# FNet mixing and a SwiGLU block in one kernel: the loads of the first two batches in another order, products of the first stage rearranged, and a new plan

## The chip, the cores and the metric

One core of a Trainium2 chip runs the whole program. Its engines are TensorE (PE, with its weight loads as PEld), VectorE (DVE), ScalarE (ACT), GpSimd (POOL) and SyncE (SP, which here issues transfers only); each works through its own queue of instructions in order, and semaphores tie the queues together. The metric is device time in microseconds of one execution. The median of 3 runs of the kernel before is 598.35 us (598.19 to 599.81).

## The reference

The input x holds 8 batches of 3008 rows of 256 numbers. Each batch goes through a two-dimensional Fourier transform of which the real part is kept; the 24,064 rows that result go through a gated feed-forward block with 1536 hidden features.

```python
X = np.fft.fft(x, axis=1)
X = np.fft.fft(X, axis=2)
x = X.real.reshape(24064, 256)
g = x @ w_gate
silu = g * (1.0 / (1.0 + np.exp(-g)))
out = (silu * (x @ w_val)) @ w_out
```

## The kernel before, in words

**What is computed where.** The transform over the 256 columns is folded into the weights: the products of CD and SDt (cosines and sines over columns) with the raw weights give Wp and Wq, and Wm is a mirrored copy of Wq with a sign. The transform over the 3008 rows is done as folds (sums and differences of rows that share a cosine) followed by matmuls with the table Tab. Its results are Pt and Qt, one pair of 128-partition tiles for each block of columns. The real transform is symmetric, so only 1504 rows of each batch are computed; each yields an output row and its mirror (the "p" and "m" halves, hp and hm).

**Tiles and units.** The 12,032 computed rows are cut into 24 tiles (480 or 512 columns, the last is shorter). A tile has 12 units of 128 hidden features. A unit makes a gate g and a value v in PSUM from Pt and Qt (line 972), turns them into sv, sp, es and sg on ScalarE and VectorE, and multiplies them to hp (VectorE, line 1186, or GpSimd, line 1192) and hm (GpSimd, line 1183, two units at a time). Then twelve such products per block of 128 rows are summed by TensorE with Wo (line 1236), copied by ScalarE (line 1243) and stored from SyncE's queue (line 1249).

**Kinds.** A string of KINDS per tile (line 928) gives each unit a digit. Bit 1 ("seeded") lets ScalarE put the even part of the value into PSUM (line 1045) and copy it back (line 1107), instead of one pass on VectorE (line 1109). Bit 2 saves one matmul of TensorE's five and costs two passes on VectorE (lines 1088 and 1152). Higher values move a product from VectorE to GpSimd. "w" is the plain form of tile 0.

**The planner.** From tile 0 on the order in each queue isn't written by hand. Sched (line 767) takes every operation with an engine, an assumed duration and the keys that it reads and writes, and puts them in order by a wished time: TensorE's assumed clock plus SHIFT for the operation's class plus BIAS for its tile and class. BIAS comes from the table BIAS_ROWS, 24 rows of 17 numbers. LAG, W_AT (when the raw weights are assumed to be there), the prices of loads in run_loads (line 1297) and the start times in the last S.run are assumptions too. The instructions themselves wait only on real semaphores; the plan decides their order.

**Batches and loads.** Each batch has a long set of rows (XA, 128 partitions) and a short one (XC, 60 partitions and a middle row). Each has "rising" rows, read as blocks of 8 (load_a) or 4 (load_c) partitions that each take four quarters of the batch, and "falling" rows in four transfers, one per quarter. Batch 0 has its own code: rises of the long set (line 258), falls (fall_a, line 261, two from ScalarE's queue and two from SyncE's), rises of the short set (rises_c, line 264), its falls (line 267). For batch 1 the short set goes to partitions 64 on, and the second of each pair of rows has to be at partitions 0 on for the fold; the rising rows are copied there on the chip (line 169), the falling ones are loaded as two half-rows each (line 164). C1_ORDER and A1_ORDER write out the order of batch 1's loads: u a rising block, d and e falls, m the middle row, c the copy. SyncE keeps at most eight transfers in flight: each issue waits for the one eight before it.

**The first stage** (batch 0, written by hand, lines 435 to 650). place (line 435) brings the rising rows into the order of the falling ones by a matmul with putA or putC; VectorE adds them crosswise (cross, cross_halves), folds them (half_fold), ScalarE casts them (half_cast, line 497), GpSimd makes the odd differences (fold_d, line 494; then EOb, line 555), and TensorE accumulates half_folded (long set) and folded_c (short set) in acc. row0 adds the first row from CEa and CEc, which heads (line 461) writes on GpSimd. ScalarE copies one half of acc to od (line 514), and first_puts (line 631) writes Pt and Qt. Between these stand first_w (line 502), the first quarter of the weight products, and load_w (line 391), the raw weights on GpSimd's queue; the weight products of the other quarters (line 1442) are units' work in tile 0.

**Later batches.** GpSimd folds each batch's sets in fold_steps (lines 178 to 202, first X to SDf), in between its products; the results feed the transforms on TensorE (line 1394).

Of the kernel before, what the change touches and what calls it, by code (L numbers as in the profile page):

```python
# [19 lines left out]
def kernel(  # L20
# [101 lines left out]
    def up_block(b, j, n):  # L122
        return rows_at(b, 2 * j - 1, [[2 * D, n], [R * D, 4], [1, 2 * D]])
# [10 lines left out]
    C1_EARLY = 6  # L134
    C1_ORDER = "uuduuduuduuduumuueuueuece"
    A1_ORDER = "uuuuduuuuduuuuduuuud"

    def load_a(b, q):
        X3 = XA.rearrange("p a q d -> p a (q d)")
        res = ([lambda h=h: q.dma_start(out=X3[LA * h:LA * (h + 1), 0:4, :],  # L140
                                         in_=up_block(b, JA - LA * h, LA)) for h in range(NA)] +
                [lambda a=a: q.dma_start(out=X3[:, 4 + a, :], in_=down_set(b, a, JA, LA, NA)) for a in range(4)])
        return in_order(A1_ORDER, u=res[:NA], d=res[NA:]) if b == 1 else res
# [5 lines left out]
    def load_c(b, q):  # L149

        X3 = XC.rearrange("p a q d -> p a (q d)")
        p0 = 64 * (b % 2)
        pm = p0 + NCR
        r = slice(p0, p0 + NCR)
        ups = [lambda h=h: q.dma_start(out=X3[p0 + LC * h:p0 + LC * (h + 1), 0:4, :],
                                       in_=up_block(b, JC - LC * h, LC)) for h in range(NC_)]
        mid = [lambda: q.dma_start(out=XC[pm:pm + 1, 0:4, 1],
                                   in_=rows_at(b, 0, [[R * D, 1], [R * D, 4], [1, D]]))]
        if b != 1:
            return ups + [lambda a=a: q.dma_start(out=X3[r, 4 + a, :], in_=down_set(b, a, JC, LC, NC_))  # L160
                          for a in range(4)] + mid

        def down(a, k):
            q.dma_start(out=XC[0:NCR, 4 + a, 0] if k else XC[r, 4 + a, 0],
                        in_=rows_at(b, R * (a + 1) - 2 * JC + k, [[2 * LC * D, NC_], [-2 * D, LC], [1, D]]))

        downs = [[lambda a=a, k=k: down(a, k) for a in range(4)] for k in range(2)]
        return in_order(C1_ORDER, u=ups, d=downs[0], e=downs[1], m=mid,
                        c=[lambda: q.dma_start(out=XC[0:NCR, 0:4, 1], in_=XC[r, 0:4, 0])])

# [99 lines left out]
    fall_a(3, nc.scalar)  # L270
    fall_a(2, q)
    fall_a(1, nc.scalar)
    fall_a(0, q)
    rises_c(q)

# [204 lines left out]

    def half_folded(eo, a0, first):
        for q in range(2):
            for a in range(a0, a0 + 2):
                dst, rhs = set_cols(acc[eo][q], Tab[:, 0, q, eo], a)
                nc.tensor.matmul(dst, EOb[:, eo, a, q, :], rhs, start=first and a == a0, stop=False, skip_group_check=True)
# [51 lines left out]
    psC = place(XC0, putC, 2, ((psO, "o"),))  # L537
    half_cast(0, 0)
    for a in range(2, 4):
        nc.scalar.copy(FA[:, a, :, P + 1:D], psA[a][:, :, P + 1:D])  # L540
    half_cast(0, 2)
    nc.scalar.activation(Z0.rearrange("p q k d -> p (q k d)"), zero.to_broadcast([P, 6 * P]), AF.Copy)
# [15 lines left out]
    cross_halves(FC[:, 0], XC0, psC, 0)  # L558
    half_fold(0, EB[:, 0, 0], FC[:, 0], psC, 0)
    folded_c(0, 0)  # L560
    copies = [first_w(0, k, 1, p_.tile([P, T], F32, name=n_)) for k, (p_, n_) in enumerate(((psG, "g"), (psV, "v")))]
    cross_halves(FC[:, 1], XC0, psC, 1)
# [7 lines left out]
    for a in range(2):  # L570
        folded_c(1, a, True)
    half_folded(1, 0, False)
    load_w(1, (1,))
    heads(Ec0[:, 0], Ec0[:, 1], CEc)
    load_w(2, (0, 1))
# [107 lines left out]
    def rows(r0, n, step):  # L683
# [7 lines left out]
    C2_AT = 39  # L691
    A1_LOAD = 8
    ROW_1 = 12
# [48 lines left out]
    )  # L742
    BIAS = {(t, k): v for t, row in enumerate(BIAS_ROWS) for k, v in zip(SHIFT, row)}
    ES_BUFS = 2
# [9 lines left out]
    WM_ACT = ()  # L754
    W_AT = (0.0, 2.0, 3.2, 4.6)
    SIGN_AT = 8
# [163 lines left out]
    def pool_us(n):  # L920
# [14 lines left out]
        "001601031052",  # L935
        "300171700001",
        "331213005030",
        "010271031001",
        "34130b310300",
        "01b300700101",  # L940
        "21312101b300",
        "001371310011",
        "32120011b212",
        "10130b135030",
        "000135003170",
        "033170001011",
        "213b21011200",
        "103b10319610",
        "4030b13300b0",
        "616404563200",  # L950
        "143034169230",
        "706150233313",
    )
# [343 lines left out]
    def run_loads(n):  # L1297
        for what, k, fn in loads[:n]:
            up = k < (NA if what[0] == "A" else NC_)
            r, w, us, ring = [], [((what[0],), k)], 0.4 if up else 0.62, 0.57 if up or what[0] == "C" else 1.14  # L1300
            if what == ("A", 1):
                r = [(("C",), C1_ORDER.rindex("u"))]
                us, ring = (0.42, 0.75) if A1_ORDER[k] == "u" else (0.75, 1.1)
            if what == ("C", 1):
                us, ring = (0.48, 0.75) if C1_ORDER[k] == "u" else (0.95, 1.0)
                if C1_ORDER[k] == "c":
                    r = [(("C",), j) for j, o in enumerate(C1_ORDER) if o == "u"]
            S.add("SP", us, fn, r=r, w=w, after=[(("A",), "pre" if A1_ORDER[k] == "d" else "preW")] if what == ("A", 1) else [],
                  lat=2.5, ring=ring)
        del loads[:n]  # L1310
# [306 lines left out]
    for i, u in enumerate(units):  # L1617
# [48 lines left out]
    owork.run(len(owork.steps))  # L1666
    S.run({'DVE': 1.6, 'ACT': 1.0, 'POOL': 1.4, 'PE': 0.0, 'SP': 2.0})

# [29 lines left out]
```

## Time and profile before

| | |
|---|---|
| median of 3 runs | 598.35 us |
| the profiled execution, in all | 600.4 us |
| its span, first to last instruction | 598.6 us |
| granted TensorE clock | 0.999 |
| moved from or to HBM | 29.43 MB read, 24.65 MB written |

Rows of a timeline give the start, the duration, the engine and line, the operation, "out<-in" by the program's names, the shape, and in brackets how long the engine had been idle before it and what ended that wait. "SPq" and "POOLq" are the issuing side of SyncE and GpSimd, "POOL ... DMA_DIRECT2D" a transfer issued by GpSimd. In windows each engine has its busy time and in brackets its number of instructions; the last columns are TensorE's granted clock, the transfer engines' mean busy share and GB/s.

### The profile page before, as it was taken

How to read it: one execution, taken by the hardware profiler on the slowest of the kernel's cores; microseconds unless marked ns; L12 is line 12 of the kernel's file. 1: busy time of each engine (PE TensorE's matmuls, PEld its weight loads, DVE VectorE, ACT ScalarE, POOL GpSimd, SP SyncE). 2: the span in 40 equal slices, each digit the busy share in tenths (PEclk: the TensorE clock that was granted, in tenths of full speed). 3: DMA queues.
4: the chain of work that ended last, by engine and by line, in shares of the span. 5: the costliest groups of instructions: out<-in, count | busy, mean ns of one | idle time of the engine just before them, and what ended most of it. 6: DMA issues, size and time to landing. Idle time of an engine off the chain costs nothing.

```text
span 598.6 us, 12468 instructions
## 1 busy us (share of the span) xinstructions
PE 587.0 (98%) x3953; PEld 389.2 (65%) x4012; DVE 570.3 (95%) x1064; ACT 557.4 (93%) x1080; POOL 527.8 (88%) x486
## 2 busy tenths in 40 slices
PE   7999999999999999999999999999999999999997
PEld 5456666666666666666666666666666666666686
DVE  8989999999999999999999999999999999999993
ACT  8778989989998999999999999999999999999995
POOL 8977999999899999998999998897986868687772
PEclk9999999999999999999999999999999999999999
DMA  9956347454715523454127122046221202111212
GB/s 247 150 110 115 109 121 141 132 140 117 178 46 107 136 70 113 123 129 138 57 55 166 46 62 82 19 115 161 63 64 37 65 19 80 48 46 53 60 54 81
DMA packets 51082, 57.65 MB, mean 96 GB/s; under 512 B 7283, under 2 KB 38439, under 8 KB 51017
## 3 DMA queue, kind: packets, MB, share of 16 engines
q1 hardware_dynamic: 47433, 53.91, 35.2%
q0 software_dynamic: 3216, 2.36, 2.8%
q8 instruction: 31, 0.51, 0.4%
q10 hardware_dynamic: 368, 0.59, 0.3%
q14 instruction: 34, 0.28, 0.2%
HBM read 29.43 MB, written 24.65 MB: 90 GB/s over the span
## 4 chain that ended last, share of the span: by engine, by line
PE 71%; ACT 8%; DMA 6%; DVE 4%; POOL 3%; issue 3%; SPq 1%; ACTq 0%; POOLq 0%; DVEq 0%
PE o L1236 30%; PE g L972 19%; PE v L972 16%; DMA XA<-in_x_dram 5%; ACT sv L1159 2%; PE o L1394 2%; PE g L1394 2%; ACT v L1045 2%; ACT es L1107 1%; POOL hm L1183 1%; DVE sv L1175 1%; ACT sp L1084 1%; DVE hp L1186 1%; ACT sp L1156 1%; ACT ev L1243 1%
## 5 line engine op out<-in xcount | busy, mean ns | idle before, releaser
L1183 POOL TENSOR_TENSOR hm<-sv 128x1024 bf16<-128x1024 f32 (+2 forms) x137 | 254.7, 1862 | 44.1 <-ACT sv L1159 17.7
L1175 DVE SCALAR_TENSOR_TENSOR sv<-es,v 128x512 f32<-128x512 f32 (+2 forms) x262 | 173.6, 668 | 5.4 <-PE v L972 2.8
L1236 PE MATMUL o<-Wo,hm 128*128 128x256 bf16 (+1 forms) x1128 | 163.6, 273 | 0.3
L1236 PE MATMUL o<-Wo,hp 128*128 128x256 bf16 (+1 forms) x1104 | 159.7, 273 | 0.2
L1186 DVE TENSOR_TENSOR hp<-sp,v 128x512 bf16<-128x512 f32 (+2 forms) x233 | 154.2, 668 | 2.8 <-PE v L972 2.0
L1236 PEld LDWEIGHTS <-hm 128*128 128x128 bf16 (+2 forms) x1140 | 111.8, 98 | 57.9 <-issue 2.5
L1236 PEld LDWEIGHTS <-hp 128*128 128x128 bf16 (+2 forms) x1140 | 111.9, 98 | 55.8 <-issue 0.9
L1159 ACT ACTIVATE sv<-g 128x512 f32<-128x512 f32 (+2 forms) x179 | 116.7, 671 | 4.6 <-PE g L972 2.3
L1084 ACT ACTIVATE sp<-g 128x512 f32<-128x512 f32 (+2 forms) x179 | 110.5, 621 | 4.1 <-PE g L972 2.7
L972 PE MATMUL v<-Pt,Wp 128*128 128x512 bf16 (+2 forms) x288 | 105.4, 375 | 1.8 <-DVE hp L1186 0.5
L972 PE MATMUL g<-Pt,Wp 128*128 128x512 bf16 (+2 forms) x280 | 104.4, 374 | 0.9 <-ACT sv L1159 0.7
L1045 ACT ACTIVATE v<-bc,w 128x512 f32<-128x512 bf16 (+2 forms) x146 | 104.6, 717 | 0.4
L1109 DVE SCALAR_TENSOR_TENSOR es<-bc,w,v 128x512 f32<-128x512 bf16 (+2 forms) x128 | 92.6, 731 | 2.4 <-ACT bc L1595 0.8
L1107 ACT ACTIVATE es<-v 128x512 f32<-128x512 f32 (+2 forms) x146 | 90.0, 618 | 3.8 <-PE g L972 1.0
L972 PE MATMUL g<-Qt,Wq 128*128 128x512 bf16 (+2 forms) x247 | 90.5, 374 | 0.4
L972 PEld LDWEIGHTS <-Wp 128*128 128x128 bf16 x576 | 56.3, 98 | 27.8 <-DVE Wp L505 0.7
L972 PE MATMUL g<-Qt,Wm 128*128 128x512 bf16 (+2 forms) x186 | 69.8, 375 | 0.2
L1088 DVE SCALAR_TENSOR_TENSOR sg<-bc,w,g 128x512 f32<-128x512 bf16 (+2 forms) x95 | 68.4, 723 | 1.4 <-PE g L972 0.7
L1159 ACT ACTIVATE sv<-sg 128x512 f32<-128x512 f32 (+2 forms) x95 | 65.1, 692 | 0.2 <-DVE sg L1152 0.2
L1152 DVE SCALAR_TENSOR_TENSOR sg<-sg,g 128x512 f32<-128x512 f32 (+2 forms) x95 | 62.9, 662 | 1.5 <-PE g L972 0.8
L1156 ACT ACTIVATE sp<-g 128x512 f32<-128x512 f32 (+2 forms) x95 | 57.7, 608 | 5.5 <-DVE sg L1152 5.3
L972 PE MATMUL v<-Qt,Wm 128*128 128x512 bf16 (+2 forms) x159 | 59.4, 374 | 0.8 <-ACT es L1107 0.4
(218 smaller groups left out, 759.1 us busy)
## 6 DMA issues: line engine op xcount, KB each, us to landing
out_dram<-ev SPq DMA_DIRECT2D x96, 128.0 KB
XA<-in_x_dram SPq DMA_DIRECT2D x30, 256.0 KB
XA<-in_x_dram SPq DMA_DIRECT2D x112, 64.0 KB
XC<-in_x_dram SPq DMA_DIRECT2D x28, 120.0 KB
XC<-in_x_dram SPq DMA_DIRECT2D x105, 32.0 KB
bc<-br SPq DMA_DIRECT2D x19, 128.0 KB
St<-Fc SPq DMA_DIRECT2D x12, 128.5 KB
out_dram<-ev SPq DMA_DIRECT2D x12, 120.0 KB
```

The lines of the kernel that those rows point to most:

```text
L972: nc.tensor.matmul(ps[:, :n], Wt[:, gv, fs], src[:, :n], start=start, stop=stop, skip_group_check=True)
L1045: nc.scalar.activation(T_[kv][:, :w], bc[t][:, :w], AF.Copy, scale=w0[:, 1, f:f + 1])
L1084: nc.scalar.activation(sp_to()[:, :w], T_[kg][:, :w], AF.Silu)
L1088: nc.vector.scalar_tensor_tensor(T_[keg][:, :w], bc[t][:, :w], w0[:, 0, f:f + 1], T_[kg][:, :w], op0=Alu.mult, op1=Alu.add)
L1107: nc.scalar.activation(T_[kes][:, :w], T_[kv][:, :w], AF.Copy, scale=2.0 if on_pool(u) > 1 else 1.0)
L1109: nc.vector.scalar_tensor_tensor(T_[kes][:, :w], bc[t][:, :w], w0[:, 1, f:f + 1], T_[kv][:, :w], op0=Alu.mult, op1=Alu.add)
L1156: nc.scalar.activation(sp_to()[:, :wp], T_[kg][:, :wp], AF.Silu)
L1159: nc.scalar.activation(sv()[:, f % 2, w - 1::-1, 1], T_[kgm if by_dve else kg][:, :w], AF.Silu)
L1175: nc.vector.scalar_tensor_tensor(sv()[:, f % 2, w - 1::-1, 0], T_[kes][:, :w], 2.0, T_[kv][:, :w], op0=Alu.mult, op1=Alu.subtract)
L1183: nc.gpsimd.tensor_tensor(hts_(t)[1][:, f - 1:f + 1, :w], sv()[:, :, :w, 1], sv()[:, :, :w, 0], op=Alu.mult)
L1186: nc.vector.tensor_tensor(hts_(t)[0][:, f, :wp], T_[ksp][:, :wp], T_[kv][:, :wp], op=Alu.mult)
L1236: nc.tensor.matmul(st["ps"][:n, j, :], hts[t][minus][:, f, c:c + n], Wo[:, f, :], start=(f == 0), stop=(f == nF - 1))
```

## The change

1. Batch 0: rises_c is issued from SyncE before the last fall of that queue. (fall_a(1) is on ScalarE's queue and stays where it is there.)
2. First stage: half_cast of the second half stands ahead of ScalarE's two copies to FA; first_w products are spread between folded_c, half_folded and row0; half_folded(1) is cut in two, each part followed by its row0; VectorE's cast of Wp for the value goes ahead of the Qt passes and turn_signs behind them; heads for CEc goes ahead of GpSimd's load of the value weights.
3. Batch 1, short set: four falls whole instead of eight half-rows, and a second on-chip copy for their second rows; the order is four rising blocks to a fall.
4. Batch 1, long set: its rising blocks are planned from unit 6 and its falls from unit 8, behind one another instead of mixed, and no longer assumed to wait for the short set. Every batch's rising blocks go 0, 4, 8, 12, 1, 5, ... instead of 0, 1, 2, ...
5. The plan: a second BIAS_ROWS stands behind the first and replaces it (all 24 rows differ), KINDS differs in 16 of the 24 tiles, and W_AT, the load prices, one lag and the last S.run's start times have other numbers.

```diff
-    C1_ORDER = "uuduuduuduuduumuueuueuece"
+    C1_ORDER = "uuuuduuuuduuuuduuudmcc"
...
-                                         in_=up_block(b, JA - LA * h, LA)) for h in range(NA)] +
+                                         in_=up_block(b, JA - LA * h, LA)) for h in (4 * (i % 4) + i // 4 for i in range(NA))] +
...
+        downs = [lambda a=a: q.dma_start(out=X3[r, 4 + a, :], in_=down_set(b, a, JC, LC, NC_)) for a in range(4)]
         if b != 1:
-            return ups + [lambda a=a: q.dma_start(out=X3[r, 4 + a, :], in_=down_set(b, a, JC, LC, NC_))
-                          for a in range(4)] + mid
-
-        def down(a, k):
-            q.dma_start(out=XC[0:NCR, 4 + a, 0] if k else XC[r, 4 + a, 0],
-                        in_=rows_at(b, R * (a + 1) - 2 * JC + k, [[2 * LC * D, NC_], [-2 * D, LC], [1, D]]))
-
-        downs = [[lambda a=a, k=k: down(a, k) for a in range(4)] for k in range(2)]
-        return in_order(C1_ORDER, u=ups, d=downs[0], e=downs[1], m=mid,
-                        c=[lambda: q.dma_start(out=XC[0:NCR, 0:4, 1], in_=XC[r, 0:4, 0])])
+            return ups + downs + mid
+        return in_order(C1_ORDER, u=ups, d=downs, m=mid,
+                        c=[lambda: q.dma_start(out=XC[0:NCR, 0:4, 1], in_=XC[r, 0:4, 0]),
+                           lambda: q.dma_start(out=XC[0:NCR, 4:8, 0], in_=XC[r, 4:8, 1])])
...
     fall_a(2, q)
+    rises_c(q)
     fall_a(1, nc.scalar)
     fall_a(0, q)
-    rises_c(q)
...
-    def half_folded(eo, a0, first):
-        for q in range(2):
+    def half_folded(eo, a0, first, qs=(0, 1)):
+        for q in qs:
...
     half_cast(0, 0)
+    half_cast(0, 2)
     for a in range(2, 4):
         nc.scalar.copy(FA[:, a, :, P + 1:D], psA[a][:, :, P + 1:D])
-    half_cast(0, 2)
...
+    copies = [first_w(0, 0, 1, psG.tile([P, T], F32, name="g"))]
     folded_c(0, 0)
-    copies = [first_w(0, k, 1, p_.tile([P, T], F32, name=n_)) for k, (p_, n_) in enumerate(((psG, "g"), (psV, "v")))]
+    copies.append(first_w(0, 1, 1, psV.tile([P, T], F32, name="v")))
...
-    half_folded(1, 0, False)
+    copies.append(first_w(1, 0, 0, psO.tile([P, T], F32, name="o")))
+    heads(Ec0[:, 0], Ec0[:, 1], CEc)
     load_w(1, (1,))
-    heads(Ec0[:, 0], Ec0[:, 1], CEc)
...
-    for i in range(2):
-        row0(0, i, acc[1][i])
     copies[0]()
     copies[1]()
+    copies[2]()
+    half_folded(1, 0, False, (0,))
+    row0(0, 0, acc[1][0])
+    od1 = even_copy(1)
+    half_folded(1, 0, False, (1,))
+    row0(0, 1, acc[1][1])
+    copies.append(first_w(1, 1, 1, psO.tile([P, T], F32, name="o")))
+    first_puts(1, od1, (0,))
+    copies[3]()
     turn_signs()
-    od1 = even_copy(1)
-    copies += [first_w(1, k, k, psO.tile([P, T], F32, name="o")) for k in range(2)]
-    first_puts(1, od1, (0,))
-    for c in copies[2:4]:
-        c()
...
-    A1_LOAD = 8
+    A1_LOAD = (6, 8)
...
-    W_AT = (0.0, 2.0, 3.2, 4.6)
+    W_AT = (0.0, 3.0, 4.0, 5.2)
...
-        "06ww20001013",
-        "031303160011",
-        "000010312133",
-        "010210112012",
+        "42ww20003010",
+        "031003330001",
+        "101330110133",
+        "010210112013",
...
             if what == ("A", 1):
-                r = [(("C",), C1_ORDER.rindex("u"))]
-                us, ring = (0.42, 0.75) if A1_ORDER[k] == "u" else (0.75, 1.1)
+                r = []
+                us, ring = (0.45, 1.0) if A1_ORDER[k] == "u" else (0.75, 1.2)
             if what == ("C", 1):
-                us, ring = (0.48, 0.75) if C1_ORDER[k] == "u" else (0.95, 1.0)
+                us, ring = (0.48, 0.7) if C1_ORDER[k] == "u" else (0.65, 1.0)
                 if C1_ORDER[k] == "c":
-                    r = [(("C",), j) for j, o in enumerate(C1_ORDER) if o == "u"]
+                    side = "u" if k == C1_ORDER.index("c") else "d"
+                    us, r = 0.95, [(("C",), j) for j, o in enumerate(C1_ORDER) if o == side]
...
-    S.add("DMA", 0.01, lambda: None, w=[(("pq", 0), "Q")], lat=0.1)
+    S.add("DMA", 0.01, lambda: None, w=[(("pq", 0), "Q")], lat=0.6)
...
-        if i == A1_LOAD:
-            loads[0:0] = ((("A", 1), k, fn) for k, fn in enumerate(load_a(1, nc.sync)))
+        if i in A1_LOAD:
+            side = "ud"[A1_LOAD.index(i)]
+            loads.extend((("A", 1), k, fn) for k, fn in enumerate(load_a(1, nc.sync)) if A1_ORDER[k] == side)
...
-    S.run({'DVE': 1.6, 'ACT': 1.0, 'POOL': 1.4, 'PE': 0.0, 'SP': 2.0})
+    S.run({'DVE': 1.4, 'ACT': 0.8, 'POOL': 1.6, 'PE': 0.0, 'SP': 2.2})
```

More of the change, by code (lines that the diff above doesn't have):

```diff
@@ L742 @@
     )
+    BIAS_ROWS = (
[24 rows of a table added]
+    )
     BIAS = {(t, k): v for t, row in enumerate(BIAS_ROWS) for k, v in zip(SHIFT, row)}
@@ L929 @@
         "wwwwwwwwwwww",
-        "06ww20001013",
-        "031303160011",
-        "000010312133",
-        "010210112012",
+        "42ww20003010",
+        "031003330001",
+        "101330110133",
+        "010210112013",
         "10110b103133",
[L935 to L938, printed above, removed]
+        "001201121052",
+        "001071610000",
+        "331213050030",
+        "001271031001",
         "34130b310300",
         "01b300700101",
-        "21312101b300",
+        "21302111b200",
         "001371310011",
         "32120011b212",
[L944 to L949, printed above, removed]
+        "10130b530000",
+        "031035003170",
+        "013370040011",
+        "203b21011210",
+        "103b10219610",
+        "0010b33700b0",
         "616404563200",
         "143034169230",
-        "706150233313",
+        "704121733213",
     )
```

24 rows, old and new, of the table BIAS_ROWS are left out of this document.

## The prediction

> **What bounds the kernel now.** I read the page's span first, then windows (busy time of each engine in a stretch), then the waits of TensorE, then the timeline around each wait.
>
> ```profile
> span 598.6 us, 12468 instructions
> ```
> ```profile
> core 0: us, PE busy (x) PEld busy (x) DVE busy (x) ACT busy (x) POOL busy (x), PEclk, DMA share, GB/s
> 18.90:61.50 42.60, 42.13 (x260) 23.80 (x263) 39.38 (x72) 34.79 (x69) 34.82 (x47) 1.00 0.70 125
> 61.50:85.50 24.00, 22.58 (x153) 15.16 (x154) 22.14 (x36) 20.98 (x42) 23.92 (x24) 1.00 0.38 112
> 85.50:111.00 25.50, 25.09 (x172) 16.52 (x172) 24.44 (x52) 22.64 (x45) 25.34 (x25) 1.00 0.69 155
> 111.00:590.00 479.00, 476.15 (x3227) 319.30 (x3277) 467.84 (x839) 462.42 (x900) 425.16 (x353) 1.00 0.33 85
> ```
>
> TensorE bounds nearly everything: from 111 to 590 us it is idle for 479.00 - 476.15 = 2.85 us, 0.6%. VectorE follows at 97.7% there. One stretch differs: from 61.5 to 85.5 TensorE is idle for 1.42 us of 24, and GpSimd is busy for 23.92 of 24, so GpSimd bounds it. It is still full (25.34 of 25.5) in the next stretch, where TensorE loses 0.41. The timeline shows how:
>
> ```profile
> 62.11 1.90 POOL L1183 TENSOR_TENSOR hm<-sv 128x1024 bf16<-128x1024 f32 x1
> ...
> 64.05 0.64 ACT L1159 ACTIVATE sv<-g 128x512 f32<-128x512 f32 x1 [0.88 <-PE g L1591]
> ...
> 64.74 0.38 PE L972 MATMUL g<-Pt,Wp 128*128 128x512 bf16 x1 [0.70 <-ACT sv L1159]
> ...
> 78.93 1.29 DVE L1175 SCALAR_TENSOR_TENSOR sv<-es,v 128x512 f32<-128x512 f32 x2 [0.71 <-POOL hm L1183]
> ...
> 80.86 0.38 PE L972 MATMUL v<-Pt,Wp 128*128 128x512 bf16 x1 [0.55 <-DVE hp L1186]
> ...
> 83.01 0.64 ACT L1159 ACTIVATE sv<-g 128x512 f32<-128x512 f32 x1 [0.99 <-POOL hm L1183]
> ```
>
> GpSimd's mirrored product (hm) keeps a buffer sv too long; ScalarE or VectorE cannot write the next sv, a PSUM tile comes free late, and TensorE waits 0.70 and 0.55. (At 64.05 the page names a matmul; the hm that ends at 64.01 fits as well.) Why GpSimd is late stands in its own queue, beside SyncE's and the chain of waits:
>
> ```profile
> 36.80 0.90 SPq L169 DMA_DIRECT2D XC<-XC  x1
> 37.94 1.42 SPq L140 DMA_DIRECT2D XA<-in_x_dram  x4
> ```
> ```profile
> 52.45 6.81 DMA XA<-in_x_dram
> ```
> ```profile
> 42.33 2.36 POOL L178 TENSOR_TENSOR SDf<-XC 128x1020 f32<-128x1020 f32 x1 [2.06 <-DMA XA<-in_x_dram]
> ...
> 44.92 0.82 POOL L1546 COPY Tab<-Tab 64x752 bf16<-64x752 bf16 x1
> ...
> 53.73 1.27 POOL L1192 TENSOR_TENSOR hp<-sp,pp 128x512 bf16<-128x512 f32 x1
> ...
> 55.72 1.89 POOL L1183 TENSOR_TENSOR hm<-sv 128x1024 bf16<-128x1024 f32 x1 [0.72 <-DVE sv L1175]
> ...
> 59.65 2.36 POOL L178 TENSOR_TENSOR SDf<-XA 128x1020 f32<-128x1020 f32 x1 [2.03 <-DMA out_dram<-ev]
> ```
>
> It idles 2.06 us for batch 1's short set (XC) and 2.03 us for its long set (XA), whose last transfer lands at 52.45 + 6.81 = 59.26; then it runs dense.
>
> **Part 1: the loads of batch 1.** Eight half-row falls become four whole ones, and a second on-chip copy is added.
>
> ```profile
> L164 SPq DMA_DIRECT2D XC<-in_x_dram x8: 836/878/922, 19.2 to 35.5; - x8
> ...
> L160 SPq DMA_DIRECT2D XC<-in_x_dram x24: 835/861/961, 65.3 to 247.2; - x24
> ...
> L140 SPq DMA_DIRECT2D XA<-in_x_dram x112: 272/298/526, 37.9 to 409.4; - x112
> ```
>
> A whole fall costs SyncE as much as a half (0.86 against 0.88), so the short set leaves 8 x 0.88 - 4 x 0.86 = 3.6 us of issue, and both copies (0.90 each) now stand behind five blocks of the long set (0.30 each). The long set's first issue moves from 37.94 up by 3.6 + 0.9 = 4.5, less about 0.9 by which part 2 starts the queue later: 34.3. Its end gains 3.6 net of start, less 1.8 for the two copies now inside it: 59.26 to about 57.5. The second copy waits for the last fall of the short set, and behind it on SyncE stand eleven blocks and all four falls of the long set, so a late fall moves the fold by as much. GpSimd is free at 55.72 + 1.89 = 57.6, so nearly all of the 2.03 goes. The copies are issued about as before (five block issues take back what they gain), so the 2.06 shrinks only by the table copy of 0.82, which now stands ahead of it. Four falls at the end of the long set, instead of one, are the risk here.
>
> ```profile
> L1186 DVE TENSOR_TENSOR hp<-sp,v 128x512 bf16<-128x512 f32 (+2 forms) x233 | 154.2, 668 | 2.8 <-PE v L972 2.0
> ...
> L1109 DVE SCALAR_TENSOR_TENSOR es<-bc,w,v 128x512 f32<-128x512 bf16 (+2 forms) x128 | 92.6, 731 | 2.4 <-ACT bc L1595 0.8
> ```
>
> GpSimd thus enters the full stretch 1.8 us earlier, and the new kinds move one product (1.27 us on GpSimd) off tile 2. That is 3 us against 1.42 + 0.41 us of idle TensorE, less what even the calm stretch loses (0.6% of 49.5 us, 0.3): 1.5 us can be won, and nothing at all at the other end. VectorE limits it: tile 2 gives it one 0.73 us pass and one product of 0.67 more, 22.14 + 1.40 = 23.5, in a stretch that would be 22.7 long. The next tile gives back three passes (2.2). I take 1.2 of the 1.5.
>
> **Part 2: the first stage.** The short set's 512 KB of rising rows pass ahead of the last 256 KB fall on SyncE's queue.
>
> ```profile
> 9.00:10.00 1.00, 1.00 (x9) 0.43 (x7) 0.91 (x5) 0.97 (x3) 0.70 (x2) 1.00 1.02 328
> ```
> ```profile
> 10.30 0.42 DVE L448 TENSOR_TENSOR FA<-v,XA 128x256 f32<-128x256 f32 x1
> ...
> 11.27 1.95 PE L435 MATMUL o<-XC,putC 128*128 128x512 f32 x4 [0.99 <-DMA XC<-in_x_dram]
> ...
> 11.42 0.41 DVE L457 TENSOR_TENSOR XA<-FA,v 128x256 f32<-128x256 f32 x1
> ...
> 11.99 0.37 ACT L540 COPY FA<-g 128x254 f32<-128x254 f32 x1 [0.76 <-DVE Eh L452]
> ...
> 12.52 0.63 ACT L497 CAST EOb<-XA 128x512 bf16<-128x512 f32 x1
> ...
> 12.96 1.10 POOL L494 TENSOR_TENSOR Fc<-FA 128x512 f32<-128x512 f32 x1
> ...
> 14.60 1.27 POOL L555 TENSOR_TENSOR EOb<-Fc 128x512 bf16<-128x512 f32 x1
> ...
> 15.81 0.73 POOL L391 DMA_DIRECT2D XA<-in_moe_w_val_dram  x1
> ...
> 16.57 0.21 POOL L461 TENSOR_TENSOR CEc<-Ec 128x2 bf16<-128x2 f32 x1
> ...
> 19.89 0.38 PE L972 MATMUL v<-Pt,Wp 128*128 128x480 bf16 x1 [0.24 <-DVE Wp L505]
> ...
> 23.26 0.24 PEld L1442 LDWEIGHTS <-CD 128*128 128x128 bf16 x2 [0.16 <-DMA XA<-in_moe_w_val_dram]
> ...
> 25.05 0.11 PEld L1442 LDWEIGHTS <-CD 128*128 128x128 bf16 x2 [0.48 <-DMA XA<-in_moe_w_gate_dram]
> ```
>
> At 328 GB/s, 256 KB take 0.8 us: the rising rows land that much sooner and TensorE's 0.99 us at 11.27 mostly goes. But the transfers are the same in sum, so the last fall now lands where the rising rows did, at about 11.2, and VectorE, which took it at 10.30, stalls 0.9. Its halves for the cast then end at 11.42 + 0.41 + 0.9 = 12.7 instead of 11.8. ScalarE now casts first (0.63) and copies to FA after that (2 x 0.37): 14.1. GpSimd's last difference waits for those copies and moves from 12.96 to 14.1; EOb behind it ends 1.1 later, and the two CEc heads (0.4) now stand ahead of the weight load issued at 15.81, which so goes out 1.5 later. Who waits for it is TensorE. TensorE's gain ends at the next gate: by 23.26 it already waits for just that weight (0.16), and at 25.05 for the next. A start that is sooner only waits longer there, with one exception: two matmuls now stand between the two waits and cover 0.2. The order of the odd products and weights (VectorE's cast of Wp now ahead of the Qt passes, which wait for ScalarE's copy od in any case) removes the 0.24 at 19.89, ahead of the same gate. Landing is not issue alone (15.81 to 23.2 is 7.4 us in a crowded stretch), so of the 1.5 I take 0.6, with 0 and 1.5 as ends; net of the 0.2, the stage costs +0.4 (-0.2 to +1.3).
>
> [...]
>
> **Part 3: the new plan.** The bias table, the kinds and the planner's prices are replaced throughout. The orders of both programs show one more 512-column matmul on TensorE (3908 to 3909 from the first gate product on), and four fewer seeds. The matmul's price stands in the chain of waits:
>
> ```profile
> 84.30 0.22 PE v L972
> ```
>
> The matmul is +0.2. A seed less takes two passes from ScalarE and gives one of 0.73 to VectorE; neither bounds a long stretch, so it is costed at nothing while VectorE stays under TensorE (R2 is the case where it does not). The 2.85 us of idle TensorE after 111 us may become less or more; I take 0, from -1 to +2.5 (as much again as all that is lost there now).
>
> **Sum:** +0.4 - 1.2 + 0.2 + 0 = -0.6 against the span of 598.6. The profiled execution, 600.4 with what lies around the span, is 2 us over the median of the runs shown, 598.35; I take the difference over to the median: 597.75. Rounded, **597.7**.
>
> **Rivals.** *Relief in full (R1):* the weights land no later (-0.2), the stretch gives 1.5 and the 2.06 wait shortens it further (tile 1's 0.47 idle of 42.6), a third of the 2.85 goes too: -0.2 - 1.5 - 0.5 - 0.9 + 0.2 = -2.9, 595.5. For it: the TensorE waits in the stretch trace back to GpSimd, which gains 3 us. Against it: VectorE's 23.5.
>
> *VectorE becomes the bound (R2, slower).* By the kinds it gets 0.65 to 0.73 more in each of tiles 6, 12, 16 and 19, and 1.4 in tile 2. Its best long share is 467.84 of 479, 97.7%; where a tile asks more than that of TensorE's time, the tile grows by the excess, and that point decides. Tile 2 then needs 23.5/0.977 = 24.1, what it takes now, so no relief comes, and each of the four later tiles grows by 0.7: 0.4 + 0 + 0.2 + 2.8 = +3.4, 601.75. For it: those 97.7%. Against it: in the two stretches from 61.5 to 111 TensorE names VectorE once (0.55), and that wait came from GpSimd.
>
> *The long set lands no sooner (R3).* Batch 1's blocks go 0, 4, 8, 12, 1, ... and the four falls come last.
>
> ```profile
> 38.00:59.00 21.00, 20.84 (x134) 13.32 (x135) 20.32 (x36) 16.75 (x32) 16.35 (x17) 1.00 0.69 123
> ```
>
> From 9 to 10 us the transfer engines moved 328 GB/s at a share of 1.02; here it is 123 at 0.69, 178 for a full share. Something other than issue slows these blocks, and an earlier issue may only queue; the transfers in flight would meet the weights too: 1.3 + 0 + 0.2 = +1.5, 599.85. [...]
>
> **How the numbers follow.** Forecast 0.36 (596.0 to 599.2 is its own range), R1 0.26, R2 0.25, R3 0.13. A measurement here tells about 0.3%, 1.8 us: 596.55 and 600.15. R1 and a quarter of the forecast lie under it: 0.35. R2 and a third of R3 lie over: 0.29. Within: 0.36. The range of 595.1 to 601.6 cuts off under half of R2 and a third of R1, some 0.2.
>
> **What would show it.** The long set's fold on GpSimd (59.65) should begin near 57.7, and TensorE's idle time between 61.5 and 85.5 fall under 0.5; the last fall should hold VectorE near 11.2; the wait for the value weights at 23.3 should grow to about 0.8. I am wrong if the fold begins where it did, if TensorE loses over 4 us after 111, or if the weights are not waited for.

## The result, and the profile after

The changed kernel takes 607.64 us, median of 4 runs (605.89 to 608.60); the kernel before took 598.69 beside it (median of 4). The ratio is 1.0144, with a 95% interval of 1.0113 to 1.0174: slower by 8.6 us. (A ratio is taken over all runs, so it need not be the quotient of the two medians, here 1.0149.) The profiled run is the shortest of the four, 605.89 with a span of 604.1.

Windows of the changed kernel, the same four stretches as in the prediction (busy time of each engine, then granted clock, transfer share, GB/s):

```profile
core 0: us, PE busy (x) PEld busy (x) DVE busy (x) ACT busy (x) POOL busy (x), PEclk, DMA share, GB/s
18.90:61.50 42.60, 41.14 (x257) 23.13 (x255) 37.77 (x73) 32.33 (x64) 33.88 (x50) 1.00 0.74 130
61.50:85.50 24.00, 23.17 (x158) 15.39 (x157) 23.00 (x38) 21.14 (x41) 23.81 (x23) 1.00 0.37 109
85.50:111.00 25.50, 24.21 (x167) 15.86 (x165) 23.80 (x51) 22.74 (x47) 25.26 (x25) 1.00 0.71 145
111.00:590.00 479.00, 477.16 (x3250) 316.25 (x3249) 465.74 (x831) 454.77 (x880) 423.84 (x353) 1.00 0.35 85
```

A second trace of the kernel before, from the later runs, in the same windows:

```profile
18.90:61.50 42.60, 42.36 (x263) 23.81 (x262) 39.63 (x74) 34.53 (x68) 34.59 (x47) 1.00 0.70 124
61.50:85.50 24.00, 22.88 (x156) 15.17 (x154) 22.19 (x37) 21.21 (x41) 23.92 (x24) 1.00 0.38 109
85.50:111.00 25.50, 25.50 (x177) 16.92 (x176) 24.65 (x52) 23.27 (x46) 25.34 (x25) 1.00 0.67 162
111.00:590.00 479.00, 478.98 (x3276) 318.92 (x3275) 467.70 (x839) 462.09 (x899) 425.34 (x354) 1.00 0.32 85
```

TensorE's idle time goes from 0.24 to 1.46 us in the first stretch, from 1.12 to 0.83 in the second, from 0 to 1.29 in the third and from 0.02 to 1.84 in the last: 4.0 of the 5.8 us between the spans (598.3 and 604.1). This second trace corrects a number of the prediction too. The 2.85 us of idle TensorE after 111 us was hardly there: the same program has 3276 matmuls on record in that window, not 3227, and 0.02 us idle. Matmuls that are missing from a trace look like idle time. The trace of the prediction has 3953 matmul records in all, this one 4012. The changed kernel's has 4013 (it has one matmul more), so its idle time can be read. Of the runs below, the first four have 3953 again; from them single waits with a named cause are read, not sums of idle time.

Where the changed kernel stands still is in its timeline, TensorE first, then the engines and the queue that it waits for:

```profile
25.11 0.59 PE L1467 MATMUL o<-XA,CD 128*128 128x512 bf16 x2 [0.96 <-DMA XA<-in_moe_w_val_dram]
...
66.75 0.38 PE L996 MATMUL g<-Pt,Wp 128*128 128x512 bf16 x1 [0.61 <-ACT sv L1183]
...
110.52 0.56 PE L996 MATMUL v<-Pt,Wp 128*128 128x480 bf16 x2 [1.28 <-ACT v L1069]
...
171.87 0.38 PE L996 MATMUL v<-Qt,Wq 128*128 128x512 bf16 x1 [1.34 <-DVE es L1133]
...
104.39 2.06 SPq L142 DMA_DIRECT2D XA<-in_x_dram  x2
...
108.86 0.59 ACT L1267 COPY ev<-o 128x512 f32<-128x512 f32 x1 [1.58 <-DMA out_dram<-ev]
...
109.80 0.67 ACT L1069 ACTIVATE v<-bc,w 128x480 f32<-128x480 bf16 x1
...
161.90 2.73 SPq L142 DMA_DIRECT2D XA<-in_x_dram  x4
...
165.31 0.56 SPq L1607 DMA_DIRECT2D bc<-br  x1
...
171.07 1.41 DVE L1133 SCALAR_TENSOR_TENSOR es<-bc,w,v 128x512 f32<-128x512 bf16 x2 [1.73 <-DMA bc<-br]
```

The two large waits have one kind of cause. At 110.52 TensorE needs a seed v, which ScalarE wrote only at 109.80, because the copy ev ahead of it (108.86) waited 1.58 for a store to free its buffer. At 171.87 it needs es, which VectorE could not make before the row bc landed, 5.2 us after its issue had ended (165.31 + 0.56). Both times SyncE had just issued the long set of a later batch (its last falls at 104.39 and 161.90). Batch 1's own long set is slow too: its last eleven blocks and its falls stand on SyncE's queue for 8.15 and 3.15 us, and GpSimd's fold begins at 61.66, not at 57.7. How much of that is the order's and how much the first stage's is read from the runs below.

```profile
42.89 8.15 SPq L140 DMA_DIRECT2D XA<-in_x_dram  x11
...
51.89 3.15 SPq L142 DMA_DIRECT2D XA<-in_x_dram  x4
...
61.66 2.36 POOL L173 TENSOR_TENSOR SDf<-XA 128x1020 f32<-128x1020 f32 x1
```

### The profile page after: what moved, and what is told of

Its sections match the earlier page's. It is cut to its first block, busy times and chain, and to the rows that moved or that the text cites. A ratio compares the mean times of both kernels' runs of the same rounds, so it can differ in the third digit from the quotient of the medians.

```text
span 604.1 us, 12496 instructions
## 1 busy us (share of the span) xinstructions
PE 592.3 (98%) x4013; PEld 388.5 (64%) x4013; DVE 571.4 (95%) x1067; ACT 552.6 (91%) x1071; POOL 526.5 (87%) x485
## 4 chain that ended last, share of the span: by engine, by line
PE 75%; DMA 13%; ACT 4%; POOL 2%; issue 2%; SPq 1%; DVE 1%; ACTq 0%; DVEq 0%; POOLq 0%
PE o L1260 33%; PE g L996 22%; PE v L996 16%; DMA XC<-in_x_dram 6%; DMA XA<-in_x_dram 4%; DMA out_dram<-ev 2%; PE g L1419 1%; PE o L1419 1%; POOL hm L1207 1%; ACT sv L1183 1%; DMA bc<-br 1%; ACT v L1069 1%; ACT es L1131 1%; PE v L1260 1%; ACT sp L1108 0%
## 5 line engine op out<-in xcount | busy, mean ns | idle before, releaser
L1210 DVE TENSOR_TENSOR hp<-sp,v 128x512 bf16<-128x512 f32 (+2 forms) x234 | 155.9, 675 | 2.9 <-PE v L996 1.9
L1183 ACT ACTIVATE sv<-g 128x512 f32<-128x512 f32 (+2 forms) x180 | 119.9, 679 | 7.6 <-POOL hm L1207 5.3
L1108 ACT ACTIVATE sp<-g 128x512 f32<-128x512 f32 (+2 forms) x180 | 112.9, 630 | 1.4 <-PE g L996 1.1
L996 PE MATMUL g<-Pt,Wp 128*128 128x512 bf16 (+2 forms) x288 | 107.2, 374 | 1.1 <-ACT sv L1183 1.1
L1069 ACT ACTIVATE v<-bc,w 128x512 f32<-128x512 bf16 (+2 forms) x142 | 102.6, 725 | 4.6 <-DVE hp L1210 3.3
L996 PE MATMUL g<-Qt,Wq 128*128 128x512 bf16 (+2 forms) x288 | 105.5, 375 | 0.0
L1133 DVE SCALAR_TENSOR_TENSOR es<-bc,w,v 128x512 f32<-128x512 bf16 (+2 forms) x132 | 96.5, 739 | 4.4 <-DMA bc<-br 1.7
L1131 ACT ACTIVATE es<-v 128x512 f32<-128x512 f32 (+2 forms) x142 | 88.6, 626 | 5.2 <-PE v L996 2.8
L996 PE MATMUL g<-Qt,Wm 128*128 128x512 bf16 (+2 forms) x194 | 72.8, 375 | 0.0
L1180 ACT ACTIVATE sp<-g 128x512 f32<-128x512 f32 (+2 forms) x94 | 57.7, 614 | 6.2 <-DVE sg L1176 6.0
L996 PEld LDWEIGHTS <-Wq 128*128 128x128 bf16 x434 | 42.4, 98 | 28.7 <-issue 2.9
```

Source lines behind the costliest of these rows:

```text
L996: nc.tensor.matmul(ps[:, :n], Wt[:, gv, fs], src[:, :n], start=start, stop=stop, skip_group_check=True)
L1069: nc.scalar.activation(T_[kv][:, :w], bc[t][:, :w], AF.Copy, scale=w0[:, 1, f:f + 1])
L1108: nc.scalar.activation(sp_to()[:, :w], T_[kg][:, :w], AF.Silu)
L1131: nc.scalar.activation(T_[kes][:, :w], T_[kv][:, :w], AF.Copy, scale=2.0 if on_pool(u) > 1 else 1.0)
L1133: nc.vector.scalar_tensor_tensor(T_[kes][:, :w], bc[t][:, :w], w0[:, 1, f:f + 1], T_[kv][:, :w], op0=Alu.mult, op1=Alu.add)
L1183: nc.scalar.activation(sv()[:, f % 2, w - 1::-1, 1], T_[kgm if by_dve else kg][:, :w], AF.Silu)
```

## The experiments

Each ratio below is against runs of the kernel before on the same chip in the same session, whose medians were 599.5 to 600.1.

**The order of the blocks, the plan and the stage, each alone or undone.** The edits, one behind the other: the old order of blocks in the changed kernel; the new order in the kernel before; the new plan in the kernel before (part 5 of the change); the old first stage in the changed kernel (parts 1 and 2).

```diff
-                                         in_=up_block(b, JA - LA * h, LA)) for h in (4 * (i % 4) + i // 4 for i in range(NA))] +
+                                         in_=up_block(b, JA - LA * h, LA)) for h in range(NA)] +
```

> The changed kernel with the rising blocks of the long set in their old order 0, 1, 2, ... again (nothing else differs). Order theory: in the changed kernel a row transfer (bc<-br) and stores (out_dram<-ev) are late while the blocks 0, 4, 8, 12, ... of batches 2 and 3 are in flight, and TensorE stands 1.28 us at 109 and 1.34 at 170 for it; with the old order both waits fall under 0.3 us each, and the time is 2.5 to 4 us below the changed kernel's 607.6. Plan theory: the waits come from where the new bias table puts row transfers and stores; the two waits stay over 1 us, the time within 1 us of 607.6.

> The kernel before with the new order of blocks (0, 4, 8, 12, 1, ...) in every batch and nothing else. Order theory: the blocks take longer to land in the plan of before too, so stores and row transfers are late there as well: 2 us or more slower than before, TensorE's new waits near 85 to 112 and 150 to 175. Plan theory: within 0.6 us of before.

> The kernel before with the new plan alone (bias table, kinds, assumed landing times, start times), loads and first stage as before. Plan theory: 3 us or more slower than before, with waits of TensorE after 100 us. Order theory: within 1.5 us of before, and no wait over 1 us at 105 to 112 or at 165 to 175.

> The changed kernel with the first stage of before (rising rows of the short set last, copies ahead of the cast, CEc heads behind the weight load, order of the products). If the weights that come 1.9 us later (25.1 instead of 23.2) cost what TensorE's wait says, the wait of 0.96 at 25 falls under 0.3, the first gate product starts at 18.9 instead of 19.5, and the time is 1.5 to 2.2 us below the changed kernel's. If a later stage takes the gain back, under 0.7 us are won.

| kernel | median, us | ratio to before (95%) |
|---|---|---|
| changed, old order of blocks | 602.07 | 1.0039 (1.0027 to 1.0051) |
| before, new order of blocks | 612.38 | 1.0206 (1.0180 to 1.0232) |
| before, new plan | 602.20 | 1.0032 (1.0019 to 1.0045) |
| changed, old first stage | 605.27 | 1.0103 (1.0073 to 1.0133) |

The order is the main cause, from both sides: one line costs the kernel before 12.6 us, and taking it out of the changed kernel gives 5.6 back (6.3 by the ratios, each of which compares runs of one session), more than the order theory asked (2.5 to 4). In the kernel before with the new order TensorE's large waits end at 68, 114 and 176; the last section shows them. With the old order (timeline and waits of that run) the same eleven blocks are issued in 5.83 us and the falls in 2.60; no row names bc<-br or a store that holds up ScalarE, and TensorE's waits at 67, 110 and 172 are gone. Its wait for the value weights is still there, at 1.93:

```profile
26.16 0.59 PE L1467 MATMUL o<-XA,CD 128*128 128x512 bf16 x2 [1.93 <-DMA XA<-in_moe_w_val_dram]
...
42.03 5.83 SPq L140 DMA_DIRECT2D XA<-in_x_dram  x11
...
48.08 2.60 SPq L142 DMA_DIRECT2D XA<-in_x_dram  x4
```

The late fold of batch 1 in the changed kernel is mostly the first stage's, not the order's. It begins at 61.66 with both, at 60.12 with the old order (first row), at 58.37 with the old first stage and the new order (second row), and at 58.01 with both undone (a run below):

```profile
60.12 2.36 POOL L173 TENSOR_TENSOR SDf<-XA 128x1020 f32<-128x1020 f32 x1
```
```profile
58.37 2.35 POOL L173 TENSOR_TENSOR SDf<-XA 128x1020 f32<-128x1020 f32 x1
```

The plan theory's 3 us are not there, though the plan alone does lose 2.4 us (1.9 by the ratio), more than the 1.5 that the order theory left it; none of its waits is over 1 us. Undoing the first stage wins 2.4, slightly more than was expected (1.5 to 2.2). The wait for the value weights is gone, as expected; the first gate product starts at 19.26, not at 18.9. With the order still new, one wait in its trace, for es behind a late row bc again, is 3.37 us long.

**Where the slow blocks meet.** Three more orders for all batches, and 0, 4, 8, 12 for batch 1 only, all in the kernel before, with an unchanged run beside them:

```diff
-    for h in range(NA)
+    for h in (4 * (i % 4) + (i // 4 + i % 4) % 4 for i in range(NA))
...
+    for h in (8 * (i // 8) + 4 * (i % 2) + i % 8 // 2 for i in range(NA))
...
+    for h in (8 * (i % 2) + i // 2 for i in range(NA))
...
+    for h in (4 * (i % 4) + i // 4 if b == 1 else i for i in range(NA))
```

> The kernel before, unchanged, for a trace from the same chip as the three runs beside it. All theories: 598 to 601 us, TensorE's longest wait after 30 us under 1 us.

> The kernel before with the blocks in the order 0, 5, 10, 15, 1, 6, 11, 12, 2, 7, 8, 13, 3, 4, 9, 14: four blocks in a row are again a quarter of the batch apart, as in 0, 4, 8, 12, but their first partitions (0, 40, 80, 120) are not multiples of 32 apart. Destination theory (blocks whose partitions differ by 32 meet at one place on the way into the on-chip memory): as fast as before, within 2 us of it. Source theory (what is slow is reading rows from far apart in device memory): as slow as with 0, 4, 8, 12, that is 10 us or more over before.

> The kernel before with the blocks in the order 0, 4, 1, 5, 2, 6, 3, 7, 8, 12, ...: each pair is 32 partitions apart, with no pair 64 apart near it. If 32 partitions apart is what meets, it is slower than before, by less than the 12.6 of 0, 4, 8, 12 (three blocks of four meet another there, two pairs here): 3 to 12 us, with TensorE's wait near 64 at 1.5 us or more. If only blocks 64 apart meet, within 2 us of before.

> The kernel before with the blocks in the order 0, 8, 1, 9, 2, 10, ...: each pair is 64 partitions apart, none in a row 32 apart. If 32 apart is what meets: within 2 us of before, or a little under it, since eight blocks in flight then reach twice as many places as 0 to 7 do. If 64 apart meets as well: 3 us or more over before.

> The kernel before with the order 0, 4, 8, 12, ... for batch 1 alone, the other six batches as before. In the run with that order for every batch TensorE stood 3.49 us at 64.7 (0.86 before), and its clock fell to 0.57 from 68 to 72. If that is batch 1's own doing, this run is 4 to 5 us slower than before and the rest of the 12.6 belongs to batches 2 to 7. If batch 1 as the prediction's third rival priced it (weights met on the way, no gain), 1 to 2 us slower. If only batches 2 to 7 matter, within 0.8 us.

| order of the blocks | median, us | ratio to before (95%) |
|---|---|---|
| 0, 5, 10, 15, 1, ... (40 partitions apart) | 600.66 | 1.0021 (1.0008 to 1.0034) |
| 0, 4, 1, 5, ... (pairs 32 apart) | 611.42 | 1.0217 (1.0182 to 1.0253) |
| 0, 8, 1, 9, ... (pairs 64 apart) | 599.90 | 1.0017 (0.9996 to 1.0039) |
| 0, 4, 8, 12, ... in batch 1 only | 604.65 | 1.0092 (1.0073 to 1.0111) |

The unchanged run took 600.10. The fold of batch 1's long set on GpSimd, one row from each timeline, in the order unchanged, spread, pairs 32 apart, pairs 64 apart, batch 1 only:

```profile
59.75 2.35 POOL L178 TENSOR_TENSOR SDf<-XA 128x1020 f32<-128x1020 f32 x1 [1.85 <-DMA out_dram<-ev]
```
```profile
60.41 2.36 POOL L178 TENSOR_TENSOR SDf<-XA 128x1020 f32<-128x1020 f32 x1 [2.93 <-DMA XC<-in_x_dram]
```
```profile
62.26 2.35 POOL L178 TENSOR_TENSOR SDf<-XA 128x1020 f32<-128x1020 f32 x1 [4.56 <-DMA out_dram<-ev]
```
```profile
59.17 2.35 POOL L178 TENSOR_TENSOR SDf<-XA 128x1020 f32<-128x1020 f32 x1 [1.50 <-DMA XC<-in_x_dram]
```
```profile
62.73 2.35 POOL L178 TENSOR_TENSOR SDf<-XA 128x1020 f32<-128x1020 f32 x1 [5.03 <-DMA out_dram<-ev]
```

The spread order reads rows from as far apart in device memory as 0, 4, 8, 12 does and costs 0.2%, so that distance by itself is not it. Pairs 32 partitions apart cost about as much as the order of the change (11.5 us against 12.6 between the medians; the ratios stand the other way round), pairs 64 apart nothing that can be told from zero. What is slow in these runs is blocks that follow one another directly and whose partitions differ by 32 (1.0206 and 1.0217, against 1.0021 at 40 and 1.0017 at 64). Standing within eight places of each other in the queue, the kernel's own limit in flight, is not enough: in 0, 1, 2, ... block 4 comes four places after block 0, 32 partitions on, and the order of pairs 32 apart has the same first eight blocks in another sequence. (The spread order, too, has blocks 32 apart four places later, 40 and 8 for one; whether its 0.2% come from them was not tested.) One rival is left. By the kernel's addresses a block is 16 KB of each quarter of the batch, so blocks 32 partitions apart are also always 64 KB apart in device memory, and no order here separates the two. Why such blocks slow each other no row here shows: that they meet at one place on the way into the on-chip memory, as the expectations have it, is the author's theory, and the runs show only which distances cost time.

Batch 1 alone costs 5.1 us, just over the range for its own doing (4 to 5). Its fold begins 3.0 us later than in the unchanged run, but TensorE loses more than that; the windows of that run say why:

```profile
68.00:72.00 4.00, 4.00 (x19) 2.31 (x18) 2.88 (x5) 3.33 (x9) 4.00 (x5) 0.64 0.38 116
72.00:76.00 4.00, 4.00 (x30) 2.73 (x28) 3.47 (x6) 3.02 (x7) 3.92 (x5) 0.94 0.43 128
```

After the wait the granted clock is 0.64 for four microseconds and 0.94 for the next four, which adds 4 x 0.36 + 4 x 0.06 = 1.7 us to the wait. TensorE's wait for sv is 3.7 us long here and 0.5 in the unchanged run: 3.2 + 1.7 = 4.9 of the 5.1.

**The parts of the first stage.** Both in the changed kernel with the old order of blocks. The first puts the rising rows back behind the last fall; the second also puts the cast behind the copies and the heads behind the weight load, so that only the order of the products is left of the new stage. The third kernel takes the whole old stage.

```diff
     fall_a(2, q)
-    rises_c(q)
     fall_a(1, nc.scalar)
     fall_a(0, q)
+    rises_c(q)
```

> The changed kernel with the old order of blocks and with the short set's rising rows behind the last fall again; the rest of the new first stage stays. With the order alone undone it was 602.07, with the whole stage undone too 599.68: 2.4 us to share out. The prediction has 1.1 of the 1.5 us by which the value weights leave later from the rising rows (VectorE's wait for the last fall) and 0.4 from the heads. By that this run is at 600.2 to 600.9, the value weights leave GpSimd near 16.5 instead of 17.58. If the casts that now stand ahead of the copies are what matters, no gain: 601.5 to 602.5.

> The changed kernel with the old order of blocks, rising rows behind the last fall, cast behind the copies and heads behind the weight load; of the new first stage only the order of the weight and odd products is left. If that order is worth what the prediction says (0.24 of a wait ahead of a gate that takes it back), the time is that of the run with the whole stage undone, 599.4 to 600.0. If it gains by itself, 598.8 to 599.3, the best version here.

> The changed kernel with the old order of blocks and the old first stage; what is left of the change is batch 1's whole falls and earlier long set, and the new plan. If the loss is the order (5.6 us) and the first stage (about 2 us) and nothing else, 599.5 to 601. If loads and plan win what the prediction gave them (1.2 us between 61.5 and 111, where TensorE's excess at starts is now near 0.2 instead of 2), up to 2 us under before. If the plan costs by itself the 2.4 us that it cost alone, 601.5 to 603.

| changed kernel, old order of blocks, and | median, us | ratio to before (95%) |
|---|---|---|
| rising rows behind the last fall | 600.93 | 1.0015 (1.0003 to 1.0027) |
| cast and heads as before too | 600.02 | 1.0013 (0.9998 to 1.0027) |
| the whole old first stage | 599.68 | 1.0004 (0.9994 to 1.0013) |

The rising rows carry most of it: 1.0039 to 1.0015, 1.4 us. In that run's timeline the value weights leave GpSimd at 16.62 and TensorE waits 0.60 for them; with cast and heads moved back as well they leave at 15.85 (third fence) and no wait for them is left. What this last step weighs is not settled: the medians of the two runs differ by 0.9 us, their ratios by 0.0002, 0.1 us.

```profile
16.62 0.73 POOL L386 DMA_DIRECT2D XA<-in_moe_w_val_dram  x1
```
```profile
24.79 0.59 PE L1467 MATMUL o<-XA,CD 128*128 128x512 bf16 x2 [0.60 <-DMA XA<-in_moe_w_val_dram]
```
```profile
15.85 0.73 POOL L386 DMA_DIRECT2D XA<-in_moe_w_val_dram  x1
```

**What of the change is worth having.** Batch 1's new loads alone in the kernel before (old order of blocks, old plan); and new loads and new plan with the blocks 0, 8, 1, 9, ... and the old first stage.

```diff
-    C1_ORDER = "uuduuduuduuduumuueuueuece"
+    C1_ORDER = "uuuuduuuuduuuuduuudmcc"
...
-    A1_LOAD = 8
+    A1_LOAD = (6, 8)
```

> The kernel before with batch 1's new loads alone (whole falls and a second copy for the short set, the long set planned from unit 6 with its falls last), old order of blocks, old first stage, old plan. The new plan alone was 1.9 us slower than before (ratio 1.0032), plan and these loads together level with it (1.0004). If the loads win what the prediction gave them whatever the plan, 598.1 to 599.1 beside 599.8. If old loads and old plan belong together as new loads and new plan do, these loads in the old plan lose too: 600.8 to 602.5.

> The changed kernel with the old first stage and the blocks in the order 0, 8, 1, 9, ...: the parts that lost are left out, and the order is one in which eight blocks reach all places. If eight blocks in flight over all places load faster than 0 to 7 do, 598.5 to 599.5 and under both kernels; if issue and in-flight limits decide, level with the order 0, 1, 2, ..., 599.4 to 600.2.

They take 600.09 us (ratio 1.0010, 0.9992 to 1.0029) and 600.00 (0.9999, 0.9989 to 1.0008). Neither theory of the first is right: the loads alone win nothing that can be told from zero, and lose nothing. The second is level with the old order, not under it. No version here beats the kernel before by what can be measured.

## Why the prediction was wrong

**The step that failed is the order of the blocks.** The sum of the forecast has no term for it. The prediction has it in one rival only: "*The long set lands no sooner (R3).* Batch 1's blocks go 0, 4, 8, 12, 1, ... and the four falls come last", at +1.5 and a chance of 0.13. By the runs it is blocks 32 partitions apart, such as 0 and 4, that slow each other there (pairs 32 apart 1.0217, pairs 64 apart 1.0017). Two things were wrong with the rival. It priced the order as a gain that does not come ("an earlier issue may only queue"), while these transfers were slower than before: the fold of batch 1 began at 62.73 instead of 59.75 with nothing else changed. And it looked at batch 1 alone, though the edit's line stands in load_a, which all batches call; the change section says so. Batch 1's share is 5.1 us of 12.6; the other batches make the rest. In the changed kernel the order costs less, 1.0144 against 1.0039, some 6.3 us: its waits are 0.61 at 67, 1.28 at 110 and 1.34 at 172, where the order alone has 3.32, 2.68 and 2.40.

**Part 2 had the right chain and too small a price.** The last fall held VectorE at 11.53 (forecast 11.2), the cast came at 13.11 (12.7), GpSimd's last difference at 14.36 (14.1), and the weight load left at 17.50, 1.7 later (1.5).

```profile
11.53 0.43 DVE L443 TENSOR_TENSOR FA<-v,XA 128x256 f32<-128x256 f32 x1 [1.12 <-DMA XA<-in_x_dram]
...
13.11 0.62 ACT L492 CAST EOb<-XA 128x512 bf16<-128x512 f32 x1 [1.87 <-DVE XA L452]
...
14.36 1.08 POOL L489 TENSOR_TENSOR Fc<-FA 128x512 f32<-128x512 f32 x1 [1.34 <-ACT FA L536]
...
17.50 0.73 POOL L386 DMA_DIRECT2D XA<-in_moe_w_val_dram  x1
```

The mis-sized term is "of the 1.5 I take 0.6". The weights' first matmul starts at 25.11, against 23.40 and 23.77 in the two traces of the kernel before, and at 26.16 in the changed kernel with the old order: 1.3 to 2.8 later for about 1.7 to 1.9 of later issue. So about all of it passed through, while single traces differ. The stage costs 1.0039 - 1.0004, 2.1 us, where the prediction had +0.4 and at most +1.3. There had been a row for it: in the trace that the prediction read, TensorE already waited for these weights (0.16 at 23.26). In the second trace it does not; but with the rising rows put back and the weights leaving 0.77 later than in the run after it (16.62 against 15.85) it waits 0.60, so little was left to hide a delay.

**Part 1 was right for the old order of blocks.** With order and stage undone the fold begins at 58.01 (forecast 57.7) and TensorE is idle for nothing between 61.5 and 85.5 (forecast under 0.5), as these two views of that run show:

```profile
58.01 2.35 POOL L173 TENSOR_TENSOR SDf<-XA 128x1020 f32<-128x1020 f32 x1
```
```profile
61.50:85.50 24.00, 24.00 (x168) 16.25 (x166) 23.81 (x39) 21.73 (x43) 22.93 (x23) 1.00 0.41 115
111.00:590.00 479.00, 478.75 (x3273) 318.18 (x3271) 467.31 (x838) 454.91 (x885) 423.84 (x353) 1.00 0.32 85
```

The fold waits for nothing there: GpSimd's product ahead of it ends at 57.96. The long set's issue begins later than the forecast's 34.3, at 34.51 in that run and at 36.05 in the changed kernel, so part 2 takes 1.5 us from it and not 0.9.

The 1.12 us of idle TensorE in that stretch went, and the time did not fall: loads and plan together stand at 1.0004. The trace of that run (4013 records, span 598.1) and the second one of the kernel before (598.3) show where most of the microsecond went. The first gate product starts at 19.52 instead of 19.14, 0.38 later; 0.23 more is idle after 111; one more matmul takes 0.22. The later start is no accident of one trace: it lies between 19.26 and 19.54 in all eight kernels here with batch 1's new loads, and between 18.86 and 19.14 in all eight traces with the old ones. Why these loads delay it is not shown, and effects of this size are at the edge of what the medians tell.

**Part 3 and the rivals.** The plan at 0 holds in the company it was made with (1.0004) and not alone (1.0032). R2 is refuted: VectorE is busy for 467.31 of 479 us there and TensorE for 478.75, so VectorE took nothing. R1 asked for 0.9 us of the 2.85 that were not there. Of the three signs that would have made the forecast wrong, one came: the fold began at 61.66, later than before, let alone at 57.7, and most of that delay is part 2's (it begins at 58.37 with the old first stage). The other two did not: TensorE is idle for 1.84 us from 111 to 590, and it waits for the value weights, 0.96 (forecast 0.8).

## What to carry to other kernels

When an edit changes an order of transfers, list every call of that line and look at what is in flight together, not only at when the first one leaves: here blocks 32 partitions apart, issued one behind the other, slowed the kernel by 2%, and rows and stores that queued behind them were late too (in the changed kernel a row by 5.2 us from its issue, and ScalarE waited 1.58 for a store). A delay of something that the bound engine had no slack for passed through: about 1.7 us of later issue cost 2.1. And a trace's idle time counts only where the number of records agrees with a second trace.

## What was not expected of the hardware

In these runs waits of TensorE of 3.32 and 2.40 us cost more than themselves and waits of 2.68 and 3.37 us did not, so the length alone does not decide it. In the timeline of the kernel before with the new order of blocks, matmuls of 512 columns take 0.63 us after a wait of 3.32, and 0.38 again from 71.97 on:

```profile
68.40 0.58 PE L972 MATMUL g<-Pt,Wp 128*128 128x512 bf16 x1 [3.32 <-ACT sv L1159]
68.78 0.63 PE L972 MATMUL g<-Qt,Wq 128*128 128x512 bf16 x1
69.21 0.63 PE L972 MATMUL v<-Pt,Wp 128*128 128x512 bf16 x1
...
71.97 0.38 PE L972 MATMUL g<-Pt,Wp 128*128 128x512 bf16 x1
...
113.77 0.36 PE L972 MATMUL v<-Qt,Wm 128*128 128x480 bf16 x1 [2.68 <-ACT es L1107]
...
176.23 0.38 PE L972 MATMUL v<-Qt,Wq 128*128 128x512 bf16 x1 [2.40 <-DVE es L1109]
```

Starts are 0.43 apart (68.78 and 69.21) where one matmul counted 0.22 in the prediction: half the clock. The wait of 2.68 at 113.77 was followed by nothing of the kind, the shorter one of 2.40 at 176.23 was. Windows of that trace, cut where the granted clock changes and at whole multiples of the same length from there, tell them apart:

```profile
64.90:68.31 3.41, 0.18 (x1) 0.00 (x0) 1.04 (x2) 0.60 (x2) 3.41 (x4) 1.00 0.33 101
68.31:71.72 3.41, 3.32 (x11) 1.78 (x11) 1.40 (x3) 2.81 (x7) 3.41 (x4) 0.50 0.35 113
109.27:112.68 3.41, 1.82 (x13) 1.15 (x12) 2.48 (x5) 0.50 (x2) 3.06 (x3) 1.00 0.92 273
112.68:116.10 3.42, 2.33 (x18) 1.66 (x18) 1.86 (x4) 3.38 (x8) 2.75 (x2) 1.00 0.49 140
174.12:177.53 3.41, 1.30 (x9) 0.87 (x9) 2.10 (x4) 2.12 (x4) 2.95 (x3) 1.00 0.46 151
177.53:180.95 3.42, 3.42 (x14) 1.68 (x12) 2.63 (x5) 1.31 (x3) 3.42 (x3) 0.50 0.01 2
```

In this trace the granted clock is 0.50 for 3.41 us at a time, and its changes fall on a fixed grid of that step: from 71.72 to 177.53 are 31 steps. Half clock followed the steps in which TensorE was busy for 0.18 and 1.30 of 3.41 us. The wait of 2.68 was cut in two by an edge of the grid; TensorE was busy for 1.82 and 2.33 in the two steps, and the clock stayed. A wait of 3.37 us in the changed kernel with the old first stage was cut in two as well and cost no clock. (That trace's clock record begins at 3.81; 48 steps on is 167.65.)

```profile
169.64 0.38 PE L993 MATMUL v<-Qt,Wq 128*128 128x512 bf16 x1 [3.37 <-DVE es L1130]
```
```profile
164.24:167.65 3.41, 2.03 (x16) 1.38 (x15) 0.85 (x2) 1.58 (x4) 0.00 (x0) 1.00 1.05 278
167.65:171.06 3.41, 1.42 (x9) 0.87 (x9) 2.22 (x4) 1.98 (x4) 2.47 (x3) 1.00 0.55 181
171.06:174.48 3.42, 3.42 (x23) 2.00 (x21) 3.42 (x7) 2.56 (x5) 3.42 (x4) 1.00 0.24 72
```

Both of these traces lack some 60 of 4000 matmul records. Two complete ones agree: with the order in batch 1 only and with pairs 32 apart, TensorE was busy for 1.27 and 1.28 us in the step ahead of the half clock. Cut into such steps, from the start of full clock to 585 us, the sixteen traces here have no other step under 1.42 us of work, and at full clock none with 1.42 or more was followed by half clock: in these runs the two kinds lie apart between 1.30 and 1.42 of 3.41 us, by busy times that are modelled. Coming back took more: with pairs 32 apart a step at half clock with 2.32 us of work was followed by another one, while the two above, with 3.32 and 3.42, were followed by full clock.

At a granted clock of 0.50 a step of 3.41 us loses half its length, 1.7 us by estimate: two of them are 3.4 of the 12.6 us of the new order in the kernel before. The unprofiled runs of the changed kernel had a granted clock of 0.997 and spans of 605.1 to 606.8, the profiled one 1.000 and 604.1. 0.3% of 605 us is 1.8 us, about one such step; that it follows one of the waits shown was not seen, since those runs have no trace.
